# ScalarE scale operands from registers, a factor of q moved to the copy of y, coefficients loaded first, and a new table of steps

## The chip, the core and the metric

The kernel runs on one core of a Trainium2 chip. The metric is the device time of one execution, in microseconds (us); lower is better. The core has a matrix engine (TensorE, PE in the profile, with its weight loads as PEld), VectorE (DVE), ScalarE (ACT), GpSimd (POOL) and SyncE (SP). DMAs are issued from SP and from POOL and run on 16 DMA engines.

## What is computed

A gated linear attention (per head a 48 x 48 state that decays with a learned gate) feeds a rational activation between two matrix products:

```python
f = 1.0 / (1.0 + np.exp(-f_logit))                # q, k, v, f_logit: (4, 8, 768, 48)
for t in range(S):
    state = f[:, :, t, :, None] * state + einsum('bhd,bhe->bhde', k[:, :, t], v[:, :, t])
    y[:, :, t] = einsum('bhd,bhde->bhe', q[:, :, t], state)
x = y.transpose(0, 2, 1, 3).reshape(3072, 384)
h = x @ w_in                                      # 384 -> 2048
P = a[0] + a[1]*h + a[2]*h**2 + a[3]*h**3
Q = 1.0 + abs(b[0])*abs(h) + abs(b[1])*h**2
out = (P / (Q + 1e-6)) @ w_out                    # 2048 -> 384, float32
```

## The kernel before

The work is cut into 12 units, one for each batch entry and each third of the sequence (256 tokens, two chunks of 128). Every unit goes through the same steps, and what each engine does, and when, is set by a table of steps called ORDER that is written out in the kernel: the program walks through it once, from left to right, and each step appends its instructions to the queues of its engines. Nothing is reordered afterwards, so an engine that waits holds up all that stands behind it in its own queue. A step is written as a name, the unit, and its range; `@` gives the PSUM slot (there are four).

The steps that matter here:

- `ld` loads q, k, f_logit (SP's queue) or v (POOL's queue); in unit 0 q, k and f come in two halves of the heads (0 2 and 2 4). `wi`, `wo` load weights in pieces (POOL's queue, four DMAs for a `wi`). `ab_` loads the coefficients a and b. POOL may have eight DMAs of its queue open; a ninth waits until the first of them has landed.
- `cz`, `ca`, `cb`, `cc` clear pads and build constant matrices. `fa` works out three numbers from b on DVE: `sig[0]`, `sig[1]`, `sig[2]`. `fb` scales a.
- Attention: `ef`, `ls` (ACT: exp and log of the gate), `cs` (PE: running sums), `A` (ACT: exp of the sums, x=0 for q and x=1 for k), `xa` (DVE: q or k times A), `T`, `Te` (PE transposes, DVE copies them out), `sc` (PE: scores), `mk` (DVE: mask), `vm` (POOL: padded copies of v), `ya`, `yb` (PE: y and the new state), `ae`, `st` (ACT and DVE: decay of the state), `ye` (ACT: copies y out of PSUM as `xT`).
- Activation: `h` (PE: x @ w_in, four blocks of 128 rows to a step), `hy` (ACT: copy of h), `sq` or `sa` (square, on DVE or ACT), `ab` (DVE: absolute value, into the tile `z`). The denominator is z plus the square: either PE adds them (`u`) and ACT takes the log from PSUM (`ln`), or they are added in SBUF, by an accumulating DMA from POOL's queue (`zd`) or by DVE (`zv`), and ACT takes the log of z (`lz`). `ex` (ACT) takes exp of minus the log. `p1`, `p2`, `pm`, `gm` (DVE), `ta` (accumulating DMA) and `tv` make the numerator and the product.
- `o` (PE: product with w_out), `oe` (ACT or DVE: copy out), `so` (store, SP's queue).

Before, the scale of the log (`ln`, `lz`) is `sig[:, 2:3]`, a column in SBUF with the same value on every partition, and q's exponential (`A` with x=0) adds the bias `sig[:, 3:4]`, the log of `sig[0]`. That log is one small ACT instruction (L264) at the end of `fa`, and it stands in ACT's queue ahead of the first `A`.

Of the kernel before, what the change touches and what calls it, by code (L numbers as in the profile page):

```python
# [19 lines left out]
cz 2; cb; ld 0 q 2 4; ld 0 v; ld 0 f 2 4; ld 0 q 0 2; ca; ld 0 k 2 4; cz 3; cz 1; ab_; ld 0 f 0 2  # L20
wi 4 8; ld 0 k 0 2; cc; cz 0; vm 0 1; ef 0 2 4; vm 0 0; ls 0 2 4; wi 0 4; ld 1 q; cs 0 2 4 @0; fa
A 0 1 2 4; ef 0 0 2; ld 1 f; xa 0 1 2 4; A 0 0 2 4; fb; wi 8 12; ls 0 0 2; xa 0 0 2 4; cs 0 0 2 @0
T 0 2 4 @1; A 0 0 0 2; Te 0 2 4; A 0 1 0 2; wi 12 16; xa 0 0 0 2; sc 0 1 @1; ld 1 k; xa 0 1 0 2
mk 0 1; T 0 0 2 @0; ya 0 0 @2 @3; Te 0 0 2; ld 1 v; ae 0; sc 0 0 @0; st 0 0; mk 0 0; ya 0 1
yb 0 2 4; st 0 1; yb 0 0 2; ld 2 q; ye 0; h 0 4 8 @2; ef 1; ld 2 f; ls 1; h 0 0 4 @3; hy 0 4 8
cs 1 @0; hy 0 0 4; h 0 8 12 @2; A 1 0; sq 0 0 8; A 1 1; p1 0 0 8; hy 0 8 12; h 0 12 16 @0; wo 4 8
xa 1 0; wo 12 16; ab 0 0 8; ld 2 k; wo 0 4; hy 0 12 16; xa 1 1; u 0 4 8 @2; wo 8 12; p2 0 0 8
T 1 @3; ln 0 4 8; p1 0 8 16; vm 1 0; ya 1 0 @0 @1; Te 1; ld 2 v; u 0 0 4 @2; ae 1; vm 1 1; ld 3 q
st 1 0; sc 1 0 @3; ln 0 0 4; ab 0 8 16; ya 1 1; mk 1 0; ld 3 f; ef 2; sc 1 1 @2; ex 0 0 8; mk 1 1
st 1 1; yb 1; sq 0 8 16; ls 2; ye 1; cs 2 @1; pm 0 0 8; u 0 12 16 @2; A 2 1; p2 0 8 16; u 0 8 12 @0  # L30
A 2 0; pm 0 8 16; ln 0 12 16; h 1 4 8 @3; ld 3 k; xa 2 0; ln 0 8 12; h 1 8 12 @2; tv 0 8 16
sa 1 4 8; h 1 12 16 @0; tv 0 0 8; hy 1 4 8; hy 1 8 12; xa 2 1; h 1 0 4 @1; hy 1 12 16; gm 0 0 8
T 2 @2; sa 1 0 4; ab 1 8 16; o 0 0 0 4 @0; sq 1 8 16; hy 1 0 4; o 0 0 4 8; ex 0 8 16; vm 2 0
o 0 1 0 4; Te 2; ld 3 v; u 1 8 12 @1; ab 1 0 8; vm 2 1; ld 4 q; u 1 12 16 @2; ln 1 8 12; p1 1 0 16
u 1 0 4 @3; ln 1 12 16; ld 4 f; gm 0 8 16; sc 2 1 @1; o 0 1 4 8; ef 3; pm 1 8 16; u 1 4 8 @2; ld 4 k
ln 1 0 4; o 0 1 8 12; mk 2 1; ls 3; o 0 0 8 12; ln 1 4 8; vm 3 1; o 0 0 12 16; p2 1 0 16; ld 4 v
cs 3 @1; ex 1 8 16; vm 3 0; o 0 1 12 16; ld 5 q; pm 1 0 8; ta 1 8 16; ya 2 0 @2 @3; ta 1 0 8; A 3 1
ld 5 f; ae 2; A 3 0; xa 3 1; ld 5 k; ef 4; st 2 0; sc 2 0 @1; xa 3 0; ya 2 1; oe 0 0 2 s; ls 4
mk 2 0; so 0 0 2; T 3 @0; ex 1 0 8; st 2 1; yb 2; Te 3; cs 4 @3; ld 6 q; vm 4 1; ye 2; ld 5 v
sc 3 0 @0; A 4 1; sc 3 1 @1; mk 3 0; vm 4 0; h 2 12 16 @2; A 4 0; mk 3 1; h 2 0 4 @3; hy 2 12 16  # L40
gm 1 8 16; ya 3 0 @1 @0; hy 2 0 4; xa 4 1; h 2 8 12 @2; sa 2 0 4; gm 1 0 8; ae 3; h 2 4 8 @3
hy 2 8 12; ld 6 f; st 3 0; xa 4 0; ef 5; ya 3 1; sa 2 4 8; ab 2 8 16; ld 6 k; T 4 @2; st 3 1; ls 5
sq 2 8 16; yb 3; hy 2 4 8; cs 5 @0; Te 4; ye 3; u 2 12 16 @3; ld 7 q; A 5 0; ab 2 0 8; h 3 12 16 @2
# [24 lines left out]
p1 6 0 16; o 4 0 4 8; ae 7; o 4 0 8 12; ls 9; zd 6 0 8; st 7 0; o 4 0 12 16; ex 5 8 16; p2 6 0 16
ya 7 1; yb 7; pm 6 8 16; oe 4 0 2 s; cs 8 @1; vm 9 0; ye 7; st 7 1; cs 9 @2; so 4 0 2; vm 9 1
pm 6 0 8; ld 10 v; A 8 1; h 7 4 8 @3; A 8 0; xa 8 1; ta 6 8 16; h 7 0 4 @0; ef 11; xa 8 0; ta 6 0 8  # L70
ld 11 k; hy 7 4 8; h 7 12 16 @1; gm 5 8 16; ld 11 q; hy 7 0 4; gm 5 0 8; A 9 0; T 8 @3; hy 7 12 16
h 7 8 12 @0; xa 9 0; A 9 1; Te 8; o 5 0 0 4 @1; lz 6 0 8; o 5 1 0 4; sq 7 0 8; sc 8 0 @3; sc 8 1 @2
mk 8 0; hy 7 8 12; o 5 1 4 8; o 5 1 8 12; ex 6 0 8; mk 8 1; o 5 0 4 8; ya 8 0 @3 @0; ab 7 8 16
lz 6 8 16; xa 9 1; o 5 0 8 12; p1 7 0 16; o 5 0 12 16; o 5 1 12 16; ae 8; ls 10; st 8 0; T 9 @2
sq 7 8 16; oe 5 0 2 s; ya 8 1; ex 6 8 16; so 5 0 2; yb 8; pm 7 0 8; cs 10 @1; vm 10 0; u 7 12 16 @0
vm 10 1; Te 9; ye 8; ld 11 v; A 10 0; h 8 0 4 @3; pm 7 8 16; ln 7 12 16; xa 10 0; h 8 12 16 @2
sa 8 0 4; ab 7 0 8; hy 8 0 4; h 8 8 12 @0; gm 6 0 8; zd 7 0 8; hy 8 12 16; p2 7 0 16; u 7 8 12 @3
hy 8 8 12; o 6 0 0 4 @2; gm 6 8 16; ta 7 8 16; ln 7 8 12; sc 9 0 @0; o 6 1 0 4; ta 7 0 8; mk 9 0
A 10 1; sc 9 1 @3; o 6 0 4 8; ex 7 8 16; mk 9 1; h 8 4 8 @1; xa 10 1; ya 9 0 @3 @0; lz 7 0 8
# [35 lines left out]
def kernel(  # L115
# [14 lines left out]
    C = 128  # L130
# [103 lines left out]
    def const_z(i):  # L234
# [13 lines left out]
        else:  # L248
            for t in states:
                zero(t)  # L250
# [337 lines left out]
```

## Time and profile before

| | |
|---|---|
| time, median of 3 runs | 240.35 us (240.1 to 240.41) |
| the profiled execution, its own time | 242.23 us |
| its span, first to last instruction | 240.5 us |
| mean granted TensorE clock | 0.984 |
| instructions | 7105 |
| PE busy | 213.5 us, 3107 matmuls |
| DVE busy | 205.7 us, 241 instructions |
| ACT busy | 206.3 us, 214 instructions |
| POOL busy | 79.4 us, 101 instructions |
| moved by DMA | 41.61 MB |

The profile follows one execution. Busy is time in which an engine executes; the idle time before an instruction is put down to what released it last. A group of instructions is named by its line of the kernel, its engine and its tiles, written as output<-inputs. Matmuls are pipelined, so a busy PE is not a PE at its peak.

### The profile page before, as it was taken

What the parts mean: (1) busy time and instruction counts of PE and PEld (TensorE: products, weight loads), DVE (VectorE), ACT (ScalarE), POOL (GpSimd) and SP (SyncE); (2) the same over time, 40 slices, a digit from 0 to 9 for tenths busy, and PEclk for the clock granted to TensorE, in tenths of its full rate; (3) what the DMA queues carried; (4) which work ended last, traced back from release to release, by engine and by line L of the source; (5) the groups of instructions that cost most, each with busy time, mean ns of one, the idle gap of its engine ahead of it and who ended that gap; (6) DMA issues with size and microseconds to landing.
All of it is one profiled execution on the core that took longest, in us unless ns stands there. A gap on an engine that the chain in (4) does not pass through costs nothing.

```text
span 240.5 us, 7105 instructions
## 1 busy us (share of the span) xinstructions
PE 213.5 (89%) x3107; PEld 148.8 (62%) x3120; DVE 205.7 (86%) x241; ACT 206.3 (86%) x214; POOL 79.4 (33%) x101
## 2 busy tenths in 40 slices
PE   0188997999899999999998999999999799999981
PEld 0065664855687766768657668667676576665540
DVE  7473299998889999989999899999999799989730
ACT  3323668999889999999999999999996999989870
POOL 8657300845120732202149525032151104322200
PEclk9999997999799999999999999999999999999999
DMA  7999999994999999999399999938929254989854
GB/s 134 221 227 230 200 204 204 224 198 34 201 208 213 173 257 216 228 231 166 59 164 200 257 198 183 238 96 107 191 69 175 47 112 92 192 159 192 182 113 121
DMA packets 62430, 41.61 MB, mean 173 GB/s; under 512 B 51520, under 2 KB 58176, under 8 KB 62400
## 3 DMA queue, kind: packets, MB, share of 16 engines
q0 software_dynamic: 21136, 22.29, 57.4%
q1 hardware_dynamic: 41264, 18.88, 32.9%
q8 instruction: 24, 0.39, 0.7%
q14 instruction: 6, 0.05, 0.1%
HBM read 25.17 MB, written 4.72 MB: 124 GB/s over the span
## 4 chain that ended last, share of the span: by engine, by line
ACT 29%; DVE 26%; PE 26%; issue 8%; DMA 8%; SPq 1%; ACTq 0%; DVEq 0%
PE hp L432 9%; ACT hy L446 7%; DMA z<-h 6%; ACT qi L498 6%; PE op L533 5%; ACT lq L474 5%; DVE qkp L311 4%; ACT lq L490 4%; DVE scm L351 4%; ACT h L454 3%; DVE gall L526 3%; PE y L364 3%; DVE z L458 2%; DMA b_sb<-in_moe_b_dram 2%; PE tp L322 2%
## 5 line engine op out<-in xcount | busy, mean ns | idle before, releaser
L432 PE MATMUL hp<-xT,w_in_sb 128*128 128x256 bf16 x576 | 70.3, 279 | 2.4 <-issue 1.1
L533 PE MATMUL op<-w_out_sb,gall 128*128 128x384 bf16 x384 | 68.8, 327 | 2.3 <-ACT lq L474 0.7
L432 PEld LDWEIGHTS <-w_in_sb 128*128 128x128 bf16 x576 | 56.6, 100 | 13.8 <-issue 3.3
L446 ACT CAST hy<-hp 128x1024 bf16<-128x1024 f32 x48 | 48.5, 1050 | 4.6 <-PE hp L432 4.4
L533 PEld LDWEIGHTS <-gall 128*128 128x128 bf16 x384 | 35.7, 98 | 26.5 <-issue 2.2
L498 ACT ACTIVATE qi<-lq 128x2048 bf16<-128x2048 f32 (+1 forms) x25 | 46.4, 1872 | 0.1
L358 POOL COPY vmp<-vn 128x128 bf16<-128x128 bf16 x24 | 24.0, 1015 | 68.1 <-PE y L364 29.0
L526 DVE TENSOR_TENSOR gall<-gall,qi 128x2048 bf16<-128x2048 bf16 (+1 forms) x25 | 29.2, 1176 | 5.3 <-ACT qi L498 4.2
L517 POOL DMA_DIRECT2D gall<-hy x23 | 20.5, 969 | 38.5 <-DVE gall L513 16.5
L351 DVE TENSOR_TENSOR scm<-sc,mask 128x1024 bf16<-128x1024 f32 x24 | 28.8, 1217 | 1.7 <-PE sc L343 1.6
L490 ACT ACTIVATE lq<-z,sig 128x2048 f32<-128x2048 bf16 x13 | 26.5, 2039 | 3.5 <-DMA z<-h 3.5
L513 DVE TENSOR_TENSOR gall<-gall,h 128x2048 bf16<-128x2048 bf16 (+1 forms) x25 | 29.2, 1176 | 0.0
L450 DVE TENSOR_TENSOR h<-hy 128x2048 bf16<-128x2048 bf16 (+1 forms) x17 | 19.8, 1164 | 8.1 <-ACT hy L446 8.1
L474 ACT ACTIVATE lq<-u,sig 128x1024 f32<-128x1024 f32 x22 | 24.7, 1138 | 0.8 <-PE u L466 0.7
L483 POOL DMA_DIRECT2D z<-h x10 | 11.2, 1119 | 35.8 <-DVE z L458 28.7
L294 PE MATMUL cs<-lsp,Ui 128*128 128x384 bf16 (+1 forms) x39 | 11.2, 353 | 11.4 <-ACT lsp L284 11.4
L503 DVE TENSOR_SCALAR gall<-hy,a_sb 128x4096 bf16<-128x4096 bf16 (+2 forms) x15 | 16.9, 1127 | 0.3 <-ACT hy L446 0.3
L458 DVE TENSOR_SCALAR z<-hy 128x2048 uint16<-128x2048 uint16 (+1 forms) x25 | 16.5, 665 | 0.6 <-ACT hy L446 0.3
L454 ACT ACTIVATE h<-hp 128x1024 bf16<-128x1024 f32 x16 | 17.0, 1060 | 0.0
L508 DVE TENSOR_SCALAR hy<-hy,a_sb 128x4096 bf16<-128x4096 bf16 (+2 forms) x15 | 16.8, 1126 | 0.0
L330 DVE COPY qkT<-tp 128x2048 bf16<-128x2048 bf16 (+1 forms) x13 | 14.8, 1136 | 2.3 <-PE tp L322 2.3
L322 PE MATMUL tp<-ident,qkp 128*128 128x128 bf16 x192 | 14.6, 235 | 0.1
(70 smaller groups left out, 288.6 us busy)
## 6 DMA issues: line engine op xcount, KB each, us to landing
gall<-hy POOLq DMA_DIRECT2D x21, 512.0 KB, 6.8
z<-h POOLq DMA_DIRECT2D x10, 512.0 KB, 6.3
qn<-in_q_dram SPq DMA_DIRECT2D x11, 384.0 KB, 10.2
fn<-in_f_logit_dram SPq DMA_DIRECT2D x11, 384.0 KB, 8.9
kn<-in_k_dram SPq DMA_DIRECT2D x11, 384.0 KB, 10.2
out_dram<-osb SPq DMA_DIRECT2D x22, 192.0 KB, 2.9
vn<-in_v_dram POOLq DMA_DIRECT2D x12, 192.0 KB, 6.9
w_in_sb<-in_moe_w_in_dram POOLq DMA_DIRECT2D x16, 96.0 KB, 6.7
```

The costliest lines, as they stand in the source:

```text
L351: nc.vector.tensor_mul(t, s["sc", g].rearrange("s r a i t -> s (r a) (i t)"), mb)
L358: nc.gpsimd.tensor_copy(s["vm"][:, :, :, 32 * x:32 * x + 16], src)
L432: nc.tensor.matmul(t[:, m - m0, :].rearrange("f (j t) -> f j t", j=UB), w_in_sb[:, kk, m * P:(m + 1) * P], s["x"][:, :, kk, :], start=(kk ...
L446: nc.scalar.copy(fl(big(s, "hy", "hy", 3), m0, m1), fl(s["hp", m0], 0, m1 - m0))
L454: nc.scalar.activation(fl(big(s, "h2", "h2", 2), m0, m1), fl(s["hp", m0], 0, m1 - m0), AF.Square)
L458: nc.vector.tensor_scalar(fl(big(s, "z", "z", 2), m0, m1).bitcast(U16), fl(s["hy"], m0, m1).bitcast(U16), 0x7FFF, None, op0=ALU.bitwise_and)
L474: nc.scalar.activation(fl(s["lq", g], m0 - 8 * g, m1 - 8 * g), fl(s["u", m0], 0, m1 - m0), AF.Ln, scale=sig[:, 2:3], bias=1.0 + 1e-6)
L490: nc.scalar.activation(fl(s["lq", g], m0 - 8 * g, m1 - 8 * g), fl(s["z"], m0, m1), AF.Ln, scale=sig[:, 2:3], bias=1.0 + 1e-6)
L498: nc.scalar.activation(fl(s["qi", g], m0 - 8 * g, m1 - 8 * g), fl(s["lq", g], m0 - 8 * g, m1 - 8 * g), AF.Exp, scale=-1.0)
L513: nc.vector.tensor_mul(fl(s["g"], m0, m1), fl(s["g"], m0, m1), fl(s["h2"], m0, m1))
L526: nc.vector.tensor_mul(fl(s["g"], m0, m1), fl(s["g"], m0, m1), fl(s["qi", g], m0 - 8 * g, m1 - 8 * g))
L533: nc.tensor.matmul(s["op"][:, j, 0:DM], s["g"][:, m, C * j:C * j + C], w_out_sb[:, m, :], start=(m == 0), stop=(m == KF - 1))
```

## The change

1. `ln` and `lz` take their scale from an ACT register, `rsig2`, that holds `sig[2]`.
2. `A` has no bias any more, for q as for k. The factor `sig[0]` is multiplied in later: `ye` becomes an ACTIVATE Copy whose scale is the register `rsig`. The small log L264 is gone, and so is `sig[3]`.
3. A new step `rg` loads the two registers from the tile `sig`. It stands between the first unit's `yb` and its `ye`.
4. `cz` clears only the pads instead of whole tiles, and the unused tile `zeros` and the unused step `warm` are gone.
5. The table ORDER is new from end to end. It has the same steps in the same number (and `rg`); each step is still on the engine that it was on. The coefficients are loaded first.

```diff
-cz 2; cb; ld 0 q 2 4; ld 0 v; ld 0 f 2 4; ld 0 q 0 2; ca; ld 0 k 2 4; cz 3; cz 1; ab_; ld 0 f 0 2
+cz 0; ca; ab_; ld 0 k 0 2; cz 2; ld 0 f 2 4; ld 0 f 0 2; cz 1; cb; cz 3; ld 0 q 0 2; ld 0 v; fa
...
+    rsig, rsig2 = (nc.alloc_register(mybir.EngineType.Activation, name=r) for r in ("rsig", "rsig2"))
...
+        for x in ((0,), (0,), (1,))[i]:
+            if i != 1:
+                nc.vector.memset(lsp[x][:, :, :, D:64].bitcast(F32), 0.0)
+            if i != 0:
+                nc.vector.memset(qkp[x].rearrange("p x i h d -> p (x i h) d")[:, :, D:64].bitcast(F32), 0.0)
+                nc.vector.memset(vmp[x][:, :, :, 16:32].bitcast(F32), 0.0)
...
-        nc.scalar.activation(sig[:, 3:4], sig[:, 0:1], AF.Ln)
+
+    def regs():
+
+        for r, i in ((rsig, 0), (rsig2, 2)):
+            nc.scalar.reg_load(r, sig[0:1, i:i + 1].bitcast(U32))
...
-        if x == 0:
-            nc.scalar.activation(t, src, AF.Exp, scale=-1.0, bias=sig[:, 3:4])
-        else:
-            nc.scalar.activation(t, src, AF.Exp, scale=1.0)
+        nc.scalar.activation(t, src, AF.Exp, scale=1.0 if x else -1.0)
...
-        nc.scalar.copy(t.rearrange("p j k t -> p j (k t)"), s["y"][:, :, 0:KD * C])
+        nc.scalar.activation(t.rearrange("p j k t -> p j (k t)"), s["y"][:, :, 0:KD * C], AF.Copy, scale=rsig)
...
-                             scale=sig[:, 2:3], bias=1.0 + 1e-6)
+                             scale=rsig2, bias=1.0 + 1e-6)
```

The last pair stands in `ln` and in `lz` alike.

The first place is ACT's queue at the start of the program, unit 0 (fn is the gate, lsp its log, cs the sums, A_180 and A_176 and so on the exponentials, alast the decay, xT the copy of y). Before:

```order
L279 ACTIVATE fn<-fn 128x384
L284 ACTIVATE lsp_90<-fn 128x4x2x48
L264 ACTIVATE sig<-sig 128x1
L306 ACTIVATE A_180<-cs 128x2x192
L279 ACTIVATE fn<-fn 128x384
L304 ACTIVATE A_186<-cs,sig 128x2x192
L284 ACTIVATE lsp_90<-fn 128x4x2x48
L304 ACTIVATE A_186<-cs,sig 128x2x192
L306 ACTIVATE A_180<-cs 128x2x192
L419 ACTIVATE alast<-sv 128x8
L414 CAST xT<-y 128x768
```

Now:

```order
L278 ACTIVATE fn<-fn 128x384
L283 ACTIVATE lsp_89<-fn 128x4x2x48
L278 ACTIVATE fn<-fn 128x384
L283 ACTIVATE lsp_89<-fn 128x4x2x48
L302 ACTIVATE A_176<-cs 128x2x192
L302 ACTIVATE A_187<-cs 128x2x192
L302 ACTIVATE A_176<-cs 128x2x192
L302 ACTIVATE A_187<-cs 128x2x192
L415 ACTIVATE alast<-sv 128x8
L268 TENSOR_LOAD sig x2
L410 ACTIVATE xT<-y 128x768
```

The log of `sig[0]` is gone from its place ahead of the first A, both halves of the gate now stand ahead of all A, and the two register loads stand just ahead of the copy of y.

The second place is POOL's queue in the same part of the program (vn is v, w_in_sb and w_out_sb the weights, vmp the padded copies of v that `vm` makes; the numbers behind the names tell the buffers apart). Before:

```order
L194 DMA vn_115<-in_v_dram 128x8x96
L201 DMA w_in_sb_104<-in_moe_w_in_dram 32x3x512 x4
L358 COPY vmp0_92<-vn_115 128x8x16 x2
L201 DMA w_in_sb_104<-in_moe_w_in_dram 32x3x512 x12
L194 DMA vn_279<-in_v_dram 128x8x96
```

Now:

```order
L195 DMA vn_141<-in_v_dram 128x8x96
L202 DMA w_in_sb_103<-in_moe_w_in_dram 32x3x512 x12
L195 DMA vn_258<-in_v_dram 128x8x96
L354 COPY vmp0_91<-vn_141 128x8x16
L202 DMA w_in_sb_103<-in_moe_w_in_dram 32x3x512 x4
L354 COPY vmp0_91<-vn_141 128x8x16
```

The first copy of unit 0's v moved behind twelve loads of w_in and the second behind all sixteen and the next unit's v.

The third place is ACT's queue in unit 6, between the point in the table where the accumulating DMA into z (`zd 6 0 8`) is issued and the log that reads it (`lz 6 0 8`, the last row of each). Before:

```order
L498 ACTIVATE qi_2633<-lq_2336 128x2048
L548 COPY osb_2730<-op_2545 128x768
L414 CAST xT_2738<-y_2573 128x768
L306 ACTIVATE A1_2752<-cs_2732 128x768
L304 ACTIVATE A0_2767<-cs_2732,sig_103 128x768
L279 ACTIVATE fn_2300<-fn_2300 128x768
L446 CAST hy_2789<-hp_2754 128x1024
L446 CAST hy_2789<-hp_2771 128x1024
L304 ACTIVATE A0_2809<-cs_2741,sig_103 128x768
L446 CAST hy_2789<-hp_2791 128x1024
L306 ACTIVATE A1_2843<-cs_2741 128x768
L490 ACTIVATE lq_2852<-z_2543,sig_103 128x2048
```

Now:

```order
L544 COPY osb_2584<-op_2439 128x768
L442 CAST hy_2450<-hp_2567 128x1024
L470 ACTIVATE lq_2636<-u_2586 128x1024
L415 ACTIVATE alast_2644<-sv_2596 128x8
L283 ACTIVATE lsp1_90<-fn_1854 128x8x2x48
L470 ACTIVATE lq_2636<-u_2638 128x1024
L486 ACTIVATE lq_2688<-z_2565 128x2048
```

Eleven instructions stood in the stretch between the two before, six stand there now.

More of the change, by code (lines that the diff above doesn't have):

```diff
@@ L103 @@
-ex 11 8 12; so 9 0 2; o 11 0 4 8; ex 11 12 16; o 11 1 0 4; gm 11 8 12; o 11 1 4 8; oe 10 0 2 s
-gm 11 12 16; o 11 1 8 12; o 11 1 12 16; so 10 0 2; o 11 0 8 12; oe 11 1 2 v; o 11 0 12 16; so 11 1 2
-oe 11 0 1 s; so 11 0 1
+cz 0; ca; ab_; ld 0 k 0 2; cz 2; ld 0 f 2 4; ld 0 f 0 2; cz 1; cb; cz 3; ld 0 q 0 2; ld 0 v; fa
+ld 0 k 2 4; wi 8 12; ef 0 2 4; cc; ld 0 q 2 4; ls 0 2 4; fb; ef 0 0 2; cs 0 2 4 @0; ls 0 0 2; ld 1 f
+A 0 0 2 4; wi 4 8; cs 0 0 2 @1; A 0 1 2 4; A 0 0 0 2; A 0 1 0 2; xa 0 0 0 2; xa 0 1 0 2; wi 0 4
@@ L106 @@
+ex 11 0 8; sq 11 12 16; ta 11 8 12; o 10 1 12 16; p2 11 12 16; u 11 12 16 @0; pm 11 12 16
+ln 11 8 12; gm 11 0 8; o 10 0 8 12; ta 11 12 16; o 10 0 12 16; ln 11 12 16; o 11 0 0 4 @2
+ex 11 8 12; o 11 0 4 8; o 11 1 0 4; ex 11 12 16; gm 11 8 12; o 11 1 4 8; oe 10 0 2 s; gm 11 12 16
+o 11 1 8 12; so 10 0 2; o 11 1 12 16; o 11 0 8 12; oe 11 1 2 v; o 11 0 12 16; so 11 1 2; oe 11 0 1 s
+so 11 0 1
 """
@@ L168 @@
     rm = consts.tile([P, 2], F32, name="rm")
-    sig = consts.tile([P, 4], F32, name="sig")
+    sig = consts.tile([P, 3], F32, name="sig")
     w_in_sb = consts.tile([P, KD, d_ff], BF16, name="w_in_sb")
     w_out_sb = consts.tile([P, KF, DM], BF16, name="w_out_sb")
+    rsig, rsig2 = (nc.alloc_register(mybir.EngineType.Activation, name=r) for r in ("rsig", "rsig2"))
     units = {}
@@ L234, in const_z @@
     def const_z(i):
+        if i == 3:
+            for t in states:
+                zero(t)
+            return
+        for x in ((0,), (0,), (1,))[i]:
[4 more added lines that the diff above has]
+                nc.vector.memset(vmp[x][:, :, :, 16:32].bitcast(F32), 0.0)
         if i == 0:
-            zero(zeros)
-            zero(lsp[0])
             nc.vector.memset(ind, 0.0)
@@ L240, in const_z @@
                 nc.vector.memset(ind[R * j:R * j + R, j:j + 1], 1.0)
-        elif i == 1:
-            zero(qkp[0])
-            zero(vmp[0])
-        elif i == 2:
-            zero(lsp[1])
-            zero(qkp[1])
-            zero(vmp[1])
-        else:
-            for t in states:
-                zero(t)
     def coef_a():
@@ L268, in coef_b @@
             nc.vector.tensor_scalar(a_sb[:, 1 + i:4], a_sb[:, 1 + i:4], sig[:, 1:2], None, op0=ALU.mult)
-    def warm(k, sl):
-        t = slot(sl, [P, 2, 512], F32, "warm")
-        for _ in range(k):
-            nc.tensor.matmul(t[:, 0, :], zeros[:, 0:P], zeros, start=True, stop=True)
     def ef(n, a0=0, a1=HP):
@@ L490, in lz @@
         nc.scalar.activation(fl(s["lq", g], m0 - 8 * g, m1 - 8 * g), fl(s["z"], m0, m1), AF.Ln,
-                             scale=sig[:, 2:3], bias=1.0 + 1e-6)
+                             scale=rsig2, bias=1.0 + 1e-6)
     def ex(n, m0, m1):
```

164 lines of the change are left out of this document (79 added, 85 removed).

## The prediction

> **What bounds the kernel now.** I read the page's busy times first, then the chain that ended last, then the engines in four stretches of the span, which separates the start and the tail from the long middle.
>
> ```profile
> PE 213.5 (89%) x3107; PEld 148.8 (62%) x3120; DVE 205.7 (86%) x241; ACT 206.3 (86%) x214; POOL 79.4 (33%) x101
> ...
> ACT 29%; DVE 26%; PE 26%; issue 8%; DMA 8%; SPq 1%; ACTq 0%; DVEq 0%
> ```
>
> ```profile
> core 0: us, PE busy (x) PEld busy (x) DVE busy (x) ACT busy (x) POOL busy (x), PEclk, DMA share, GB/s
> 0.00:22.00 22.00, 8.70 (x174) 6.59 (x175) 13.49 (x40) 6.14 (x13) 15.83 (x35) 1.00 1.10 203
> 22.00:40.00 18.00, 15.70 (x226) 10.77 (x227) 11.60 (x14) 12.93 (x15) 2.58 (x4) 0.95 1.31 204
> 40.00:230.00 190.00, 183.79 (x2678) 128.74 (x2689) 178.69 (x185) 183.76 (x184) 60.96 (x62) 0.99 0.88 170
> 230.00:240.50 10.50, 5.34 (x32) 2.75 (x29) 1.94 (x3) 3.44 (x5) 0.00 (x0) 0.95 0.45 112
> ```
>
> The chain changes hands between ACT, DVE and PE, a good quarter each. In the middle, 40 to 230 us, ACT is busy 183.76 of 190 us, so it idles 6.2 us; DVE idles 11.3. The first 22 us are different: no engine is full there, and what counts is the order in which loads land. So the change has two fields: ACT's time in the middle, and the latency of the start.
>
> **Scales from registers.** ACT's groups in the middle stretch, one row for each line and shape:
>
> ```profile
> L446 ACT CAST hy<-hp 128x1024 bf16<-128x1024 f32 x44 | 44.5, 1054 | 1.2 <-PE hp L432 1.0
> L498 ACT ACTIVATE qi<-lq 128x2048 bf16<-128x2048 f32 x22 | 42.5, 1944 | 0.1
> L490 ACT ACTIVATE lq<-z,sig 128x2048 f32<-128x2048 bf16 x13 | 26.5, 2039 | 3.5 <-DMA z<-h 3.5
> L474 ACT ACTIVATE lq<-u,sig 128x1024 f32<-128x1024 f32 x20 | 22.5, 1140 | 0.0
> L454 ACT ACTIVATE h<-hp 128x1024 bf16<-128x1024 f32 x16 | 17.0, 1060 | 0.0
> L304 ACT ACTIVATE A<-cs,sig 128x768 f32<-128x768 f32 x10 | 9.4, 942 | 0.0
> L414 ACT CAST xT<-y 128x768 bf16<-128x768 f32 x11 | 9.1, 826 | 1.1 <-PE y L364 1.0
> L306 ACT ACTIVATE A<-cs 128x768 f32<-128x768 f32 x10 | 8.5, 854 | 0.6 <-PE cs L294 0.6
> ...
> L419 ACT ACTIVATE alast<-sv 128x8 f32<-128x8 f32 x10 | 2.1, 212 | 0.0
> ```
>
> The two A lines differ only in the operand sig: 942 - 854 = 88 ns. The same size shows where a log with sig stands beside an instruction of its length without it: 1140 - 1060 = 80 ns (L474 and L454, both from PSUM), 2039 - 1944 = 95 ns (L490 and L498). The change takes sig out of all three: 10 x 88 + 20 x 80 + 13 x 95 = 0.88 + 1.60 + 1.24 = 3.7 us of ACT's middle. The copy of y turns from a CAST into an ACTIVATE; L454 against L446 says 1060 - 1054 = 6 ns each, 11 times, under 0.1 us. An operand read from a register occurs nowhere in this trace. Its price lies between nothing (a constant in the instruction, as in L306) and a whole smallest ACT instruction, 212 ns (L419); I take nothing, because a constant is the nearer thing to it, and keep the upper end for a rival. The two register loads stand where ACT waited 3.58 us for y anyway (row at 21.19 below), so I cost them at nothing; without that cover they would cost twice 0.2 us by the same L419 row. For register loads from HBM, the Trainium skill (Runtime: NRT & Kernel Launch, section "Instruction fetch mechanics") states some 200 ns each; these come from SBUF, no run here shows one, and by that figure the sum would be the same, as the wait covers 0.4 us.
>
> Does ACT's 3.7 us become time? ACT idles only 6.2 of 190 us there, so I count it in full in the likeliest case; DVE's 11.3 us of idle time is the room that it needs.
>
> **The accumulating DMAs (`zd`).** 3.5 of ACT's 6.2 us idle are waits for z before a log (L490 above). These rows show how:
>
> ```profile
> z<-h POOLq DMA_DIRECT2D x10, 512.0 KB, 6.3
> ```
>
> ```profile
> DMA to landing us min/median/max: 4.5/6.3/10.9
> ```
>
> ```profile
> 178.97 0.84 POOL L483 DMA_DIRECT2D z<-h  x1
> ...
> 185.71 2.00 ACT L490 ACTIVATE lq<-z,sig 128x2048 f32<-128x2048 bf16 x1 [2.12 <-DMA z<-h]
> ```
>
> ```profile
> 213.80 2.01 ACT L490 ACTIVATE lq<-z,sig 128x2048 f32<-128x2048 bf16 x1 [0.61 <-DMA z<-h]
> ...
> 223.73 2.00 ACT L490 ACTIVATE lq<-z,sig 128x2048 f32<-128x2048 bf16 x1 [0.81 <-DMA z<-h]
> ```
>
> ```profile
> 45.59 2.87 ACT L446 CAST hy<-hp 128x1024 bf16<-128x1024 f32 x3
> ```
>
> From issue to landing takes 4.5 us at best and 6.3 in the median, and the log waits when ACT has less work than that in between. The work is counted from the table: the ACT steps between `zd` and its `lz`, each at its mean duration less about 0.14 us, since neighbours overlap (three hy in 2.87 us: (2.87 - 1.05) / 2 = 0.91 for one of 1.05). Units 2 to 11 before: 8.7, 13.1, 6.5, 8.9, 9.6, 5.3, 4.3, 6.5, 5.3, 6.2 us. The waits were at units 8, 10 and 11, all among the four smallest (4.3, 5.3, 6.2), so the count sees them. The new table gives 4.0, 6.7, 5.3, 8.6, 4.5, 4.5, 9.3, 5.7, 3.4, 4.3 us. The wait at unit 8 goes (9.3), but units 2, 6, 7, 10 and 11 now have 4.5 or less; unit 6 is the third place shown above. With 0.4 us added for the way ACT lags behind the table (in the trace unit 8 had 185.71 - 2.12 - 178.97 = 4.6 against 4.3 counted), the shortfalls add up to 9.6 us at a landing of 6.3, and to 0.8 at 4.5. I take 6.0, nearer the upper end, because the three waits seen fit 6.3 or more. That is 2.5 us more than the 3.5 before; ends -2.7 and +6.1.
>
> The accumulations into gall (`ta`) come nearer to their readers on DVE too; I cost that at nothing, under cover of DVE's 11.3 us idle.
>
> **The start.** The rows of unit 0:
>
> ```profile
> 2.95 0.52 SPq L209 DMA_DIRECT2D b_sb<-in_moe_b_dram  x1
> ...
> 4.35 0.52 ACT L279 ACTIVATE fn<-fn 128x384 f32<-128x384 f32 x1 [2.26 <-DMA fn<-in_f_logit_dram]
> ...
> 6.25 0.52 ACT L284 ACTIVATE lsp<-fn 128x384 bf16<-128x384 f32 x1 [1.38 <-DVE ind L238]
> ...
> 8.91 0.22 DVE L255 TENSOR_SCALAR bm<-b_sb 128x2 uint32<-128x2 uint32 x1 [2.51 <-DMA b_sb<-in_moe_b_dram]
> ...
> 10.25 0.20 ACT L264 ACTIVATE sig<-sig 128x1 f32<-128x1 f32 x1 [3.48 <-DVE sig L261]
> 10.36 0.47 ACT L306 ACTIVATE A<-cs 128x384 f32<-128x384 f32 x1
> ...
> 16.32 2.24 POOL L201 DMA_DIRECT2D w_in_sb<-in_moe_w_in_dram  x4 [2.56 <-DMA w_in_sb<-in_moe_w_in_dram]
> ...
> 19.68 0.30 PE L364 MATMUL y<-scm,vn 64*32 64x128 bf16 x4
> ...
> 21.19 0.80 ACT L414 CAST xT<-y 128x768 bf16<-128x768 f32 x1 [3.58 <-PE y L364]
> ...
> 22.04 5.28 PE L432 MATMUL hp<-xT,w_in_sb 128*128 128x256 bf16 x24 [0.90 <-ACT xT L414]
> ```
>
> ACT stood still for 3.48 us until b had landed and sig was there. That wait goes, for two reasons: b is first in SP's queue, and no A needs sig. What is late next is f. It was second in SP's queue and is now fourth (b, a, k ahead of it), so it is issued near 2.4 us. Its own landing before took 3.0 us; the k that was fourth before took 6.1:
>
> ```profile
> DMA to landing us min/median/max: 3.0/3.0/3.0
> ```
>
> ```profile
> DMA to landing us min/median/max: 6.1/6.1/6.1
> ```
>
> So the first `ef` comes at 5.4 to 8.5 us, and four ACT instructions of about 0.45 us pitch later the first A, at 7.2 to 10.3, that is 0 to 3.2 us earlier than 10.36. On DVE, however, the second half of q's `xa` now stands behind the first state update and mask:
>
> ```profile
> L351 DVE TENSOR_TENSOR scm<-sc,mask 128x1024 bf16<-128x1024 f32 x24 | 28.8, 1217 | 1.7 <-PE sc L343 1.6
> ...
> L423 DVE TENSOR_TENSOR state<-sv,alast 128x384 bf16<-128x384 f32 x20 | 11.0, 552 | 3.8 <-ACT alast L419 2.4 <-PE sv L390 1.3
> ```
>
> That puts 1.2 + 0.6 = 1.8 us into the chain to y. Net: from 1.4 us earlier to 1.8 later. f has one load of q's size ahead of it as before, so I take a landing near 4 us, and the first `h` 0.3 us earlier. On POOL, the copies of v move behind the loads of w_in (the second place above). Eight DMAs can be open; a w_in load waited 2.56 us for that at 16.32 before. If v is issued about 1.8 us later than before, the last of the sixteen waits for a slot until about 17 to 18 us, and the second copy ends near 18.6, a us before `yb` (19.68). I cost it at nothing; that cover is thin, and up to 1 us is kept for the upper end. Smaller memsets save DVE time only where it waits.
>
> **The sum.** 240.35 - 3.7 + 0.1 + 2.5 - 0.3 = 238.95, so 239.0 us. The profiled execution took 242.23 with a span of 240.5, 1.9 above the median of the runs; the differences are taken from its span and put to the median.
>
> **Rivals.**
> - Everything comes out well: the ACT time in full and no more waits for z than before. 240.35 - 3.6 - 0.3 = 236.4; with 1.2 us fewer waits, 235.2. For it: ACT is the fullest engine beside PE. Against it: the short stretches ahead of `lz`.
> - ACT's time isn't worth anything, because DVE sets the pace: DVE's work is unchanged, and it is on the chain 26%. Only the start is left: 240.05, no measurable change. Against it: 11.3 us of DVE idle. The Trainium skill (Perfetto Trace Analysis, section "Identifying the Most-Contended Engine") takes the engine with the highest occupancy as the one to optimize, and says that matmul busy time is a poor measure, weight-load time a better one; by that rule ACT and DVE are level at 86%, PE has room at 62%, and the end would be this rival's.
> - Slower: the waits for z reach their upper end, 9.6 us. 240.35 - 3.6 - 0.3 + 6.1 = 242.55. It decides once the waits exceed what the scales give: 3.9 more than the 3.5 of before, 7.4 in all, which a landing of some 5.8 us in the five short stretches would nearly give.
> - The change doesn't do what it says: the register operand costs time. At 100 ns for each of 44 instructions (11 + 20 + 13) that is 4.4 us, and 239.0 becomes 243.4; 34 ns each already cancel the gain.
>
> **Chances.** Likeliest case 0.40 (its own range 238.0 to 239.8); all well 0.22; DVE sets the pace 0.14; waits for z 0.18; register operand 0.06. A change of 0.2%, 0.5 us, is about what a measurement of this kernel can tell. Faster: 0.40 + 0.22, 0.62. The same: the DVE case, 0.14. Slower: 0.18 + 0.06, 0.24. The range runs from the good case, 235.4, to near the slow one, 242.2; outside stay the register case, part of the waits and the best of the good case, under 0.2.
>
> **What would show it.** The logs and A at 1060, 1945 and 855 ns; if they stay at 1140, 2040 and 940, the first step is wrong. The copy of y near 830 ns. ACT's waits for z: 6 us in sum at units 2, 6, 7, 10, 11. The first `h` between 20.6 and 23.8. The forecast is wrong if the middle stretch doesn't shorten although ACT is less busy, or if POOL's copies of v hold up `yb`.

## The result, and the profile after

The changed kernel is slower: 247.75 us (median of four runs, 246.87 to 250.23) against 240.22 us for the kernel before in the same comparison (239.04 to 240.41). The ratio is 1.0341, with a 95% interval of 1.0257 to 1.0425. The medians here are of all runs, while the ratios compare fast executions with fast ones, so a ratio need not be the quotient of two medians. The profiled execution took 248.27 us with a span of 246.6. The prediction, 239.0 with a range of 235.4 to 242.2, was wrong, in sign too.

The page's busy times and its chain after the change:

```profile
PE 213.8 (87%) x3104; PEld 146.9 (60%) x3120; DVE 205.8 (83%) x240; ACT 203.3 (82%) x213; POOL 72.2 (29%) x101
...
PE 27%; DMA 25%; DVE 21%; issue 13%; ACT 11%; POOL 1%; SPq 1%; ACTq 0%; DVEq 0%
DMA z<-h 14%; PE hp L428 9%; DMA gall<-hy 9%; PE op L529 8%; DVE qkp L307 3%; ACT qi L494 3%; DVE gall L509 3%; ACT hy L442 3%; DVE scm L347 3%; DVE gall L522 3%; PE y L360 2%; DVE z L454 2%; ACT lq L486 2%; DVE qkT L326 2%; DVE state L419 2%
```

ACT does 3 us less work (203.3 for 206.3), as the change intends, and PE and DVE do the same as before. Yet DMA on the chain goes from 8% to 25%, and 23% of the span now lies in two kinds of transfer: the accumulations into z and into gall. The stretches say where the time went:

```profile
core 0: us, PE busy (x) PEld busy (x) DVE busy (x) ACT busy (x) POOL busy (x), PEclk, DMA share, GB/s
0.00:22.00 22.00, 10.10 (x180) 7.26 (x181) 11.53 (x39) 7.12 (x13) 13.61 (x32) 1.00 1.08 185
22.00:40.00 18.00, 15.22 (x229) 10.05 (x230) 13.98 (x16) 13.27 (x16) 6.23 (x10) 0.92 1.26 215
40.00:230.00 190.00, 178.55 (x2646) 124.46 (x2657) 173.78 (x176) 174.19 (x178) 50.56 (x57) 0.99 0.86 167
230.00:246.60 16.60, 9.96 (x55) 5.16 (x54) 6.47 (x11) 8.71 (x8) 1.81 (x2) 0.97 0.57 124
```

In the middle all three computing engines stand still more than before: ACT 15.8 us (before 6.2), DVE 16.2 (11.3), PE 11.5 (6.2). The granted clock there is 0.99 both times. What ACT waited for is in its groups, here over the whole span (busy time and mean length of one, then idle time and what ended it), and DVE's wait for gall in the fence after them:

```profile
L302 ACT ACTIVATE A<-cs 128x768 f32<-128x768 f32 x22 | 17.2, 825 | 2.1 <-PE cs L293 2.0 <-DVE qkp L307 0.2
L410 ACT ACTIVATE xT<-y 128x768 bf16<-128x768 f32 x12 | 9.8, 820 | 7.8 <-PE y L360 7.6
L470 ACT ACTIVATE lq<-u 128x1024 f32<-128x1024 f32 x22 | 22.4, 1034 | 3.1 <-PE u L462 3.1
L486 ACT ACTIVATE lq<-z 128x2048 f32<-128x2048 bf16 x13 | 25.1, 1931 | 12.8 <-DMA z<-h 12.8
```

```profile
DVE gall L522 <- DMA gall<-hy: 5.4, 5, 2.8
```

The second fence is a row of the waits: 5.4 us in total, 5 times, 2.8 at the longest. The 7.6 us that the copy of y waited for y are one wait in the start, which ended at 19.96 us (3.58 us before the change). The instructions with a register as scale are as short as predicted or a little shorter: 1034 and 1931 ns for the logs (before 1140 and 2039), 820 for the copy of y; A, which has lost its bias, takes 825. But the logs of z wait 12.8 us instead of 3.5, and the product with gall 5.4 us; before, that row read

```profile
DVE gall L526 <- DMA gall<-hy: 1.1, 2, 0.7
```

### The profile page after: what moved, and what is told of

It reads as the page before. It is cut to its first block, busy times and chain, and to the rows that moved or that the text cites. A ratio compares the mean times of both kernels' runs of the same rounds, so it can differ in the third digit from the quotient of the medians.

```text
span 246.6 us, 7103 instructions
## 1 busy us (share of the span) xinstructions
PE 213.8 (87%) x3104; PEld 146.9 (60%) x3120; DVE 205.8 (83%) x240; ACT 203.3 (82%) x213; POOL 72.2 (29%) x101
## 4 chain that ended last, share of the span: by engine, by line
PE 27%; DMA 25%; DVE 21%; issue 13%; ACT 11%; POOL 1%; SPq 1%; ACTq 0%; DVEq 0%
DMA z<-h 14%; PE hp L428 9%; DMA gall<-hy 9%; PE op L529 8%; DVE qkp L307 3%; ACT qi L494 3%; DVE gall L509 3%; ACT hy L442 3%; DVE scm L347 3%; DVE gall L522 3%; PE y L360 2%; DVE z L454 2%; ACT lq L486 2%; DVE qkT L326 2%; DVE state L419 2%
## 5 line engine op out<-in xcount | busy, mean ns | idle before, releaser
L428 PE MATMUL hp<-xT,w_in_sb 128*128 128x256 bf16 x576 | 71.4, 279 | 5.6 <-ACT xT L410 2.4
L513 POOL DMA_DIRECT2D gall<-hy x23 | 21.3, 1074 | 62.5 <-DVE hy L504 22.3
L522 DVE TENSOR_TENSOR gall<-gall,qi 128x2048 bf16<-128x2048 bf16 (+1 forms) x25 | 29.8, 1192 | 9.3 <-DMA gall<-hy 5.4
L486 ACT ACTIVATE lq<-z 128x2048 f32<-128x2048 bf16 x13 | 25.1, 1931 | 12.8 <-DMA z<-h 12.8
L354 POOL COPY vmp<-vn 128x128 bf16<-128x128 bf16 x24 | 16.9, 726 | 35.1 <-DMA vn<-in_v_dram 21.4
L470 ACT ACTIVATE lq<-u 128x1024 f32<-128x1024 f32 x22 | 22.4, 1034 | 3.1 <-PE u L462 3.1
L479 POOL DMA_DIRECT2D z<-h x10 | 9.4, 945 | 40.9 <-DVE z L454 14.2
L302 ACT ACTIVATE A<-cs 128x768 f32<-128x768 f32 (+1 forms) x26 | 18.9, 774 | 2.2 <-PE cs L293 2.0
L195 POOL DMA_DIRECT2D vn<-in_v_dram x12 | 12.3, 1022 | 19.6 <-issue 19.5
L318 PE MATMUL tp<-ident,qkp 128*128 128x128 bf16 x192 | 13.7, 226 | 3.8 <-DVE qkp L307 3.8
```

The lines of the kernel that those rows point to most:

```text
L428: nc.tensor.matmul(t[:, m - m0, :].rearrange("f (j t) -> f j t", j=UB), w_in_sb[:, kk, m * P:(m + 1) * P], s["x"][:, :, kk, :], start=(kk ...
L470: nc.scalar.activation(fl(s["lq", g], m0 - 8 * g, m1 - 8 * g), fl(s["u", m0], 0, m1 - m0), AF.Ln, scale=rsig2, bias=1.0 + 1e-6)
L486: nc.scalar.activation(fl(s["lq", g], m0 - 8 * g, m1 - 8 * g), fl(s["z"], m0, m1), AF.Ln, scale=rsig2, bias=1.0 + 1e-6)
L513: nc.gpsimd.dma_start(out=fl(s["g"], m0, m1), in_=fl(s["hy"], m0, m1), accum_op=ALU.add)
L522: nc.vector.tensor_mul(fl(s["g"], m0, m1), fl(s["g"], m0, m1), fl(s["qi", g], m0 - 8 * g, m1 - 8 * g))
```

## The experiments

Theory W: the new table leaves the accumulating DMAs too little time, and the waits for z and gall are the loss. Theory R: the edits themselves disturb. Theory P: the new order is worse for some other reason. The kernel before ran beside each group on the same chip (medians 239.81, 240.78, 240.06, 240.46 and 239.7), so between groups the ratios to it are compared. "Old table" is the order of the kernel before, "new table" that of the change.

**Edits and table apart.** e1 is the changed code with the old table (`rg` put in ahead of `ye 0`); e2 is the old code with the new table.

```diff
 e1: code of after,  ORDER of before:  -ye 0;   +rg; ye 0;
 e2: code of before, ORDER of after:   -rg;
```

> All edits to the code, with the table of steps of before (the register loads put in ahead of the first copy of y). Theory W (the new table leaves the accumulating DMAs too little time, and the waits for z and gall are what was lost): the edits alone are a gain, 240.2 - 3.6 of ScalarE time = 236.6, within 235.5 to 238.5, waits of ScalarE for z about 3.5 us as before. Rival R (the edits disturb, by register operands or the moved factor): 243 or more. Rival P (the new table is worse for reasons other than these DMA waits): 236.6 as well.

> The new table of steps with the code of before (column operands, log of sig as bias). Theory W: slower than the changed kernel by part of the 3.7 us that the edits save, 249 to 252. Rival R: 240 to 243. Rival P: 249 to 252.

e1: 239.6 us, ratio 0.9972 (0.9936 to 1.0008), no change that can be measured; no theory had that, W and P expected a gain (236.6) and R a loss. e2: 252.6 us, just above the 249 to 252 of W and P, ratio 1.0549 (1.0495 to 1.0603). So the table alone costs 5.5%, and R is out: under the new table the edits save 0.021 x 240 = 5.0 us. Under the old table they save next to nothing, although ACT's busy time falls there as well, to 203.0 us. The chain of e1 by engine, and two rows of its waits:

```profile
PE 59%; DVE 14%; ACT 12%; issue 6%; DMA 5%; SPq 1%; POOL 0%; DVEq 0%; ACTq 0%; POOLq 0%
```

```profile
ACT lq L486 <- DMA z<-h: 3.0, 3, 1.8
...
DVE gall L522 <- DMA gall<-hy: 2.4, 2, 1.5
```

With ACT relieved, most of the chain is PE's (59%, before 26%): it has 212 us of matmuls, and the start and the end in which it can't run. The waits were 3.0 us for z and 2.4 for gall.

**One cause taken away.** e3: zd accumulates into a spare tile, so the log doesn't wait for it; the bytes are moved as before, the sum is missing from the result. e4: ta is not issued at all, which leaves out half of the polynomial.

```diff
 e3: -nc.gpsimd.dma_start(out=fl(s["z"], m0, m1), in_=fl(s["h2"], m0, m1), accum_op=ALU.add)
     +nc.gpsimd.dma_start(out=fl(scr, 0, m1 - m0), in_=fl(s["h2"], m0, m1), accum_op=ALU.add)
 e4: -nc.gpsimd.dma_start(out=fl(s["g"], m0, m1), in_=fl(s["hy"], m0, m1), accum_op=ALU.add)
     +return
```

> The changed kernel, but the accumulating DMA of the denominator writes to a spare tile, so that its traffic stays and no log waits for it; the sum in z is left out for these halves. Theory W: 12.8 us of ScalarE waits go, worth 6 to 10 us: 238 to 242. Rival P: 246 to 248, the waits only move to other places. Rival R: 247 to 248.

> The changed kernel without the accumulating DMAs into gall (half of the numerator's sum is left out). Theory W: 5.4 us of VectorE waits for gall go, and the z transfers behind them land sooner (one of 10.7 us and one of 10.2 stood behind two of these): 242 to 245. Rival P: 246 to 248. Rival R: 247 to 248.

e3: 247.7 us, 1.0328 (1.0295 to 1.0361), nothing gained, as P had it and not W: the wait had moved, to 9.9 us for gall (before 5.4; this profile is of the fastest of its runs, 244.74). e4: 242.81 us, 1.011 (1.007 to 1.0151), about two thirds of the loss gone, but it takes away transfers as well as a wait, so it doesn't tell the two apart.

**First attempt at the waits alone.** e5 sends ta to two spare tiles; e6 also lets the log read h squared instead of z, so that nothing waits for an accumulating DMA; e7 is e6 under the old table. One output buffer instead of two made room for the spare tiles. e9 moves a load behind ta of unit 1.

```diff
 e5: -out=fl(s["g"], m0, m1)            +out=fl(scr[m0 // 8], 0, m1 - m0)
     -name="osb")                       +name="osb", bufs=1)
 e6, e7: e5 and  -fl(s["z"], m0, m1), AF.Ln    +fl(s["h2"], m0, m1), AF.Ln
 e9: -ld 5 v; ... vm 4 0; ... vm 4 1; ... ta 1 8 16    +ta 1 8 16; ld 5 v; vm 4 0; vm 4 1
```

> The changed kernel with all its DMAs, but the accumulating DMA of the second polynomial half (ta) writes to two spare tiles instead of gall, so the product with gall (gm) does not wait for it; one output buffer instead of two makes room. Left out: that half of the polynomial in the result. If the waits for these DMAs are what the table cost on DVE (theory W), about as much comes back as in the run without the DMAs at all (242.8), so 242 to 244; the waits for z stay. If the traffic of these DMAs, not the wait, was what cost time there (theory T), it stays at 246 to 248. If the table is worse for another reason (theory P), also 246 to 248.

> As the run before, and the logarithm that reads z (lz) reads h squared instead, so that no accumulating DMA is awaited by a computing engine; all of them still run. Left out: both sums. Theory W (the new table leaves the two kinds of accumulating DMA too little time, and both waits together are the whole loss): 238 to 241, level with the changed code under the old table (239.6). Theory P (the table itself is worse, whatever is awaited): 245 or more. In between, 242 to 244: about half each.

> Control for the run before: the changed code under the old table, with the same two edits. The waits of that run were 3.0 us for z and 2.4 us for gall, beside a TensorE that is on the chain for 59%. Theory W: 237.5 to 239.6, at most 2 us gained, since TensorE sets the pace. If the edits help every table alike (theory P), it falls as far below 239.6 as the run before falls below 247.7.

> The changed kernel with the load of v of unit 5 and two copies on GpSimd (ld 5 v, vm 4 0, vm 4 1) put behind the second accumulating DMA of unit 1 (ta 1 8 16), so that the 12 us for which GpSimd's queue stood at that load no longer hold back the accumulations of unit 1. If this standstill is what made unit 1 and all units after it late (theory Q): 245.5 or less. If the inputs of the accumulation came that late anyway (theory W; they were ready within 1.6 us of its issue): 247 to 248, no change that can be measured.

e5: 248.43 us, 1.0319 (1.0232 to 1.0406), where W expected 242 to 244. e6: 239.37 us, 0.996 (0.9934 to 0.9986): the whole loss is gone. But the control e7 came out at 243.25, 1.0084 (1.0047 to 1.0121), slower than the old table with its waits, which neither theory allows; the waits of its trace point to the single output buffer:

```profile
DVE osb L545 <- DMA out_dram<-osb: 6.0, 1, 6.0
...
PE op L530 <- DVE osb L545: 4.9, 1, 4.9
```

e9 gained nothing (248.97; 1.0321, 1.0236 to 1.0406), so the 12 us for which POOL stood at that load are not the cause (rows of the changed kernel). In e9 POOL stood 16.15 us ahead of the same accumulation instead and issued it at 63.88 us (62.22 in the changed kernel): its inputs were no earlier.

```profile
60.03 1.11 POOL L195 DMA_DIRECT2D vn<-in_v_dram  x1 [12.16 <-issue]
...
62.22 1.82 POOL L513 DMA_DIRECT2D gall<-hy  x2
```

**The reverse: the old table with late DMAs.** e8, e11 and e12 keep e1 and only put `zd`, `ta` or both later in its table, until they stand as near to their readers as in the new one. For example:

```diff
 e8, e12: -ta 3 8 16 with 11.5 us of VectorE's work ahead of its gm    +the same step with 6.1 us
 e8, e11: -zd 3 0 8 with 13.1 us of ScalarE's work ahead of its lz     +the same step with 6.3 us
```

> The changed code under the old table (239.6), with nothing moved but the accumulating DMAs: each zd and ta is put later in the table, until no more work of the waiting engine lies between it and its reader than the new table has there (counted in work: ScalarE's between zd and lz, VectorE's between ta and gm). Those with less than 6 us: 8 of 10 zd, 14 of 23 ta (before the move 3 and 5; the new table 7 and 11). Theory W (too little work behind the DMAs is the loss, whatever else the new table does): 245 to 249, with waits for z of 8 us or more or for gall of 5 us or more. Theory P (something else in the new order, which these runs of the old order don't have): at most 242.

> As the run before, but zd alone is moved later; ta stays where the old table has it. If one late kind of DMA is enough, as the runs with one of the two waits taken away say (247.7 and 248.4 under the new table): 243 to 247. If the loss needs both: 239.5 to 241.

> As the run before the last, but ta alone is moved later; zd stays where the old table has it. If one late kind is enough: 243 to 247. If the loss needs both: 239.5 to 241. VectorE has more idle time than ScalarE, so if the two differ, this one is the cheaper.

e8: 245.03 us, 1.0204 (1.0121 to 1.0287). e11: 245.32, 1.02 (1.0131 to 1.0269). e12: 244.97, 1.0214 (1.0145 to 1.0283). So the distance alone costs 2%, whatever else is in the table, and one late kind is as bad as two: the costs don't add. The expectation that gall would be the cheaper was not borne out; the two are level. ACT's waits for z in e8 were few and long, 7.2 us in three places (expected 8 or more), and DVE's for gall 3.9 (expected 5 or more). The rows of the waits, of e8, e11 and e12 in this order:

```profile
ACT lq L491 <- DMA z<-h: 7.2, 3, 4.3
```

```profile
ACT lq L491 <- DMA z<-h: 7.9, 4, 4.6
...
DVE gall L527 <- DMA gall<-hy: 2.7, 2, 2.0
```

```profile
DVE gall L527 <- DMA gall<-hy: 5.1, 3, 2.5
ACT lq L491 <- DMA z<-h: 5.1, 2, 3.8
```

In e11 only the wait for z grew against e1 (3.0 and 2.4 there). In e12 both grew, although only `ta` was moved, so the loss of e12 can't be put down to gall alone.

**A version for both.** e10 is e1 with another order of unit 0's loads.

```diff
 -cz 2; cb; ld 0 q 2 4; ld 0 v; ld 0 f 2 4; ld 0 q 0 2; ca; ld 0 k 2 4; cz 3; cz 1; ab_; ld 0 f 0 2
 +cz 2; cb; ld 0 f 2 4; ld 0 f 0 2; ld 0 q 2 4; ld 0 k 2 4; ld 0 q 0 2; ld 0 k 0 2; ab_; ld 0 v; ca; cz 3; cz 1
 -... cs 0 2 4 @0; fa; A 0 1 2 4; ...        +... xa 0 1 0 2; fa; fb; mk 0 1; ...
```

> An attempt at a version that beats both: the changed code under the old table (239.6), with the loads of unit 0 in another order on SyncE's queue (both halves of f first, then q, k, q, k, and a and b last) and the coefficients computed behind unit 0's products, since no A needs them any more. In that run the second half of f was issued at 3.97 us and took 6.6 us to land, which stood on the chain, and the first matrix product of unit 0 began at 21.9. If the second half of f was what the start waited for, it begins 1 to 3 us earlier and the time is 236.5 to 238.5. If k or the weights then land as late as f did: 239 to 240, no change that can be measured.

e10: 239.95 us (236.74 to 243.82), inside the 239 to 240 that was named for no change; the ratio, 0.9945 (0.9896 to 0.9994), is just under 1. The first product with w_in comes at 20.25 (row below) instead of 21.86 in e1's trace, but the profiled execution took 239.94, as long as e1's 239.78: 1.6 us at the start did not reach the end. In that trace the waits were 5.2 us for z and 4.0 for gall, 3.8 more in sum than in e1's, which may be where they went; no run shows it.

```profile
20.25 4.81 PE L432 MATMUL hp<-xT,w_in_sb 128*128 128x256 bf16 x24 [0.91 <-ACT xT L414]
```

**What the output buffer costs.** e13 is e1 and e14 the changed kernel, each with one output buffer and all waits kept.

```diff
 -ms.tile([P, UB, DM], F32, name="osb")      +ms.tile([P, UB, DM], F32, name="osb", bufs=1)
```

> The changed code under the old table with one output buffer instead of two, all waits kept: what the control run (old table, no accumulating DMA awaited, 243.25) had besides. In that run VectorE waited 6.0 us for the last store to leave the one buffer, and TensorE 4.9 us behind it. If the single buffer is what made the control slow: 242.5 to 245. If not (taking the waits away harms the old table): 239 to 241, and the reading of the pair of runs without waits becomes doubtful.

> The changed kernel with one output buffer instead of two, all waits kept: what the runs with spare tiles under the new table had besides. If the single buffer costs nothing there: 247 to 249, and the runs without the wait for gall (248.4) and without both waits (239.4) are read as they stand. If it costs 3 to 5 us here too: 251 to 253, and taking away the wait for gall alone did bring something.

e13: 243.64 us, 1.0108 (1.0042 to 1.0174); e14: 255.07 us, 1.0573 (1.0492 to 1.0654), above both of its ranges. By the ratios the buffer costs 0.0136 x 240 = 3.3 us under the old table and 0.0232 x 240 = 5.6 under the new one. It explains the control e7, and it had spoiled e5 and e6: held against e14, e5 gains about 6 us and not nothing. In e14 the granted clock was lower too (0.954 in the profiled execution, 0.984 in the changed kernel's); what part of the 5.6 and the 6 us that is stays open.

**The clean set.** Both output buffers, no spare tiles. ta accumulates hy onto itself (e15), the log reads h squared (e18), both (e16), both under the old table (e17). In e15 and e16 ta no longer waits for the first half of the polynomial either, which in the changed kernel was a wait of 0.8 us.

```diff
 e15: -out=fl(s["g"], m0, m1), in_=fl(s["hy"], m0, m1)    +out=fl(s["hy"], m0, m1), in_=fl(s["hy"], m0, m1)
 e18: -fl(s["z"], m0, m1), AF.Ln                          +fl(s["h2"], m0, m1), AF.Ln
```

> The changed kernel with both output buffers; ta accumulates hy onto itself instead of into gall (same bytes, same queue, no spare tiles), so gm doesn't wait for it. Left out: that half of the polynomial. Late gall is one of the two causes and either wait alone holds the pipeline: 246 to 248. If the single output buffer had hidden a gain in the first such run, as its price of 7.3 us (255.07 against 247.75) says: 240 to 243.

> The changed kernel, zd into z as it is, but lz reads h squared, so that ScalarE doesn't wait for z. Left out: that sum. The first such run (247.7) sent all zd to one spare tile, where each had to wait for the one before. If z alone is not the cause: 246.5 to 248. If the spare tile had hidden a gain: 243 to 245.5.

> Both of these edits, both output buffers. With one output buffer it was 239.37. If that buffer cost it as much as it cost the old table (4.0 us): 235 to 236.5. If it cost nothing because nothing was late: 239 to 239.5. In both cases all of the loss is gone, and it lies in the two waits together.

> Control: the same two edits under the old table, both output buffers. The old table with its waits: 239.6; with one output buffer, taking the waits away brought 0.4 us (243.64 to 243.25). TensorE sets the pace there: 238.5 to 239.6. If waits cost there too: 236 to 238.

| new table | time, us | ratio to before |
|---|---|---|
| both awaited (the change) | 247.75 | 1.0341 (1.0257 to 1.0425) |
| z alone awaited (e15) | 245.19 | 1.0211 (1.0143 to 1.0279) |
| gall alone awaited (e18) | 246.89 | 1.0304 (1.0239 to 1.0369) |
| neither awaited (e16) | 236.18 | 0.9863 (0.9798 to 0.9927) |

Either wait alone keeps most of the loss (0.035 x 240 = 8.4 us for z, 0.044 x 240 = 10.6 for gall, where both make 11.5), and only without both is it gone. So it is W, in a stronger form than I had it. For e15 I had named 246 to 248 or 240 to 243, and it fell between the two; e18 and e16 fall into ranges given. P is out: without the waits the new order is faster than the kernel before by 1.4%, with all the transfers still running. The transfers landed no sooner there (median 7.0 us for z and 7.7 for gall in e16, 6.5 and 6.6 in the changed kernel), so it is the waiting that cost, not the traffic.

e17 has no interval: its four runs took 237.38, 237.94, 241.0 and 244.24 us, with a median of 239.47 (e1: 239.6). By the lower two the waits cost some 2 us under the old table as well; two runs are too few to say so.

The traces of e15 and e18 show what one wait does alone. The first row is of e15's waits, the second of e18's; then the chain of e18 by engine and by line, the chain of e16 by engine, and the middle stretch of e16 (columns as above):

```profile
ACT lq L486 <- DMA z<-h: 9.3, 6, 2.7
```

```profile
DVE gall L522 <- DMA gall<-hy: 10.1, 7, 2.8
```

```profile
DVE 41%; PE 21%; DMA 17%; issue 15%; ACT 2%; SPq 1%; POOL 1%; DVEq 0%; ACTq 0%; POOLq 0%
DMA gall<-hy 13%; PE hp L428 8%; PE op L529 7%; DVE gall L509 7%; DVE gall L522 6%; DVE scm L347 5%; DVE qkp L307 4%; DMA kn<-in_k_dram 4%; DVE h L446 3%; DVE gall L499 3%; DVE qkT L326 3%; DVE z L454 3%; DVE hy L504 3%; DVE state L419 3%; PE y L360 2%
```

```profile
PE 66%; DVE 16%; ACT 6%; issue 4%; DMA 4%; SPq 1%; ACTq 0%; DVEq 0%
```

```profile
40.00:230.00 190.00, 186.54 (x2778) 129.54 (x2776) 180.33 (x189) 183.42 (x187) 54.83 (x59) 1.00 0.89 176
```

gm needs both: qi, which comes from z by `lz` and `ex`, and gall, which comes from ta. When ACT no longer waits for z (e18), DVE waits for gall twice as long as in the changed kernel (10.1 us for 5.4), so most of what is gained on one side is lost on the other. The reverse is not so plain: in e15 the waits for z did not grow (9.3 us for 12.8), and yet 8.4 us of loss remain. How the rest is shared out stays open. In e16 nothing of the kind is left, PE is on the chain for 66% and idles 3.5 of the middle 190 us.

## Why the prediction was wrong, point by point

**Scales from registers, -3.7: right for the single instruction, wrong as time.** All lengths came as predicted or 10 to 30 ns shorter. ACT's busy time fell by less than the lengths: 22 x 104 + 13 x 108 + 11 x 113 ns make 4.9 us over the whole span, and it fell by 3.0 (3.3 in e1), probably because neighbours overlap, as three hy in 2.87 us do. "I count it in full in the likeliest case" is a step that failed: under the old order e1 has the relief and no gain that can be measured, and PE makes up 59% of the chain. Only under the new order, where ACT is waited for, did the edits bring time (5.0 us, e2 against the change). My rival for that, that DVE sets the pace, had the right outcome for the edits under the old order and the wrong engine. The Trainium skill (Perfetto Trace Analysis, section "Identifying the Most-Contended Engine") judges the room left on TensorE by MFU, the share of its peak arithmetic that is used, and by the share of weight loads, not by matmul time. On weight loads e16 disagrees: they fill 62% of its span, and yet PE is 66% of its chain; MFU was not worked out here.

The two register loads were longer than the 212 ns each that I had taken from the smallest ACT instruction, 286 and 470 ns:

```profile
L268 ACTq TENSOR_LOAD <-sig x2: 286/378/470, 12.2 to 12.8; - x2
```

They lie at the head of the 7.57 us for which ACT waited for y, so their cost of nothing was right.

**The waits for z, +2.5: the term that was mis-sized.** It was +9.3 (12.8 after, 3.5 before). The waits, in the order of units 2, 3, 6, 7, 9, 10 and 11:

```profile
79.38 1.91 ACT L486 ACTIVATE lq<-z 128x2048 f32<-128x2048 bf16 x1 [3.12 <-DMA z<-h]
98.47 1.91 ACT L486 ACTIVATE lq<-z 128x2048 f32<-128x2048 bf16 x1 [2.61 <-DMA z<-h]
149.79 1.92 ACT L486 ACTIVATE lq<-z 128x2048 f32<-128x2048 bf16 x1 [2.02 <-DMA z<-h]
175.70 1.91 ACT L486 ACTIVATE lq<-z 128x2048 f32<-128x2048 bf16 x1 [1.21 <-DMA z<-h]
208.19 1.92 ACT L486 ACTIVATE lq<-z 128x2048 f32<-128x2048 bf16 x1 [0.86 <-DMA z<-h]
214.34 1.91 ACT L486 ACTIVATE lq<-z 128x2048 f32<-128x2048 bf16 x1 [0.82 <-DMA z<-h]
230.73 1.92 ACT L486 ACTIVATE lq<-z 128x2048 f32<-128x2048 bf16 x1 [2.21 <-DMA z<-h]
```

The five units that I named add up to 3.12 + 2.02 + 1.21 + 0.82 + 2.21 = 9.4 us. At the median landing of 6.3 us my count gave them 8.8 (the other 0.8 of my upper end, 9.6, are units 4 and 9), so the count was near; I took 6.0, between the two ends. Unit 9 waited 0.86 us where the count had 0.2, and unit 4 not at all. Unit 3 waited 2.61 us and was not in the count: its transfer took 98.47 - 87.79 = 10.7 us, the longest of all, which a count with one landing time can't see:

```profile
87.79 0.84 POOL L479 DMA_DIRECT2D z<-h  x1 [2.17 <-PE sc L339]
```

```profile
DMA to landing us min/median/max: 5.1/6.5/10.7
```

**The accumulations into gall, costed at nothing: the step that failed.** I wrote that they come nearer to their readers on DVE and took "cover of DVE's 11.3 us idle", without counting. Counted afterwards as I had counted z, the table leaves less than 6 us of DVE's work in 11 of 23 places, before in about 5. The idle time was no cover either: in the middle stretch before the change, DVE's waits were for ACT and PE (the longest 2.0 us, for alast) and only 1.1 us in all for gall. What the runs showed in its place: DVE waited 5.4 us for gall, and with the wait for z taken away (e18) this wait alone costs 10.6 us.

**The sum itself.** I added waits on ACT and on DVE to the time like separate amounts. They meet in one instruction, gm, and e15, e18, e8, e11 and e12 all show that the amounts don't add: 12.8 and 5.4 us of recorded waits cost 11.5 us together, and either wait alone 8 to 11.

**The start, -0.3.** The first `h` came at 20.82 in the profiled execution (22.04 before), within 20.6 to 23.8; in e16, with the same table, at 22.97, since f and one half of k landed later there (the first exponential waited for f until 6.41 us, in the changed kernel's trace until 5.84). This is no part of the loss. The copies of v held up nothing.

**The rivals.** The slower one, waits for z at the upper end, had the right mechanism and place; its 242.55 lacked units 3 and 9 and gall. "Everything comes out well", 236.4, is what e16 shows for this table without the two waits: 236.18. The register operand costs no time.

## What to carry to other kernels

When an order is changed, count for every asynchronous step how much work lies between it and its first reader, for each engine that reads, and hold that against the slow landings of the trace, not the median. When two waits feed the same instruction, removing one may show little until the other is gone too, so try them singly and together. And what an experiment gives up to make room (here an output buffer) needs a run of its own before its result is read.

## What the runs showed that was not expected

- One output buffer instead of two costs 3.3 us under the old table and 5.6 under the new one by the ratios (4.0 and 7.3 by the medians), the latter at a lower granted clock. With no accumulating DMA awaited it costs 0.0097 x 240 = 2.3 (e6 against e16).
- The slow landings of the accumulations of 512 KB into z were gone in e4, which has no ta. There they took

```profile
DMA to landing us min/median/max: 4.5/5.4/6.3
```

  with a slowest of 6.3 instead of 10.7 us. Whether ta itself or the order that it left made the difference, no run shows.
